# Dependencies that hold back loads of the front, wide fp32 products as TensorE's fillers, and an epsilon kept in a second column, in a kernel of attention, experts and slots

## The chip, the cores and the metric

The kernel runs on one core of a Trainium2 chip. Its engines are TensorE (PE, whose weight loads the profile lists as PEld), VectorE (DVE), ScalarE (ACT), GpSimd (POOL) and SyncE (SP), which here issues every transfer. The metric is the device time of one run in microseconds; lower is better. Of several runs the median counts.

## The reference

Three stages follow each other. Attention runs over 4 batches, 8 heads, 576 positions of 64 numbers and is the sum of two parts: one over queries, keys and values averaged over groups of 4 positions (144 of them), one over a band of positions less than 4 apart. Its output is a table of 2304 tokens by 512. A layer of width 2048 with a rational function follows, and then a soft mixture of 8 experts with 4 slots each.

```
def sm_attn(qq, kk, vv):
    s = scale * np.matmul(qq, kk.transpose(0, 1, 3, 2))
    s = s - np.max(s, axis=-1, keepdims=True)
    a = np.exp(s)
    a = a / (np.sum(a, axis=-1, keepdims=True) + 1e-09)
    return np.matmul(a, vv)
out_up = np.repeat(sm_attn(q_d, k_d, v_d), factor, axis=2)
attn_out = out_up + out_local              # out_local: banded, |i-j| < 4
...
h = x @ w_in
P = a[0] + a[1] * h + a[2] * h * h + a[3] * h * h * h
Q = 1.0 + np.abs(b[0]) * np.abs(h) + np.abs(b[1]) * h * h
x = (P / (Q + 1e-06)) @ w_out
...
logits = x @ phi
slot_input = softmax_over_tokens(logits).T @ x
slot_out[e] = np.maximum(slot_input[e] @ w1[e], 0.0) @ w2[e]
return softmax_over_slots(logits) @ slot_out
```

## The kernel before

Attention works on pairs of heads: 4 pairs for each of 4 batches, 16 in all. For a pair the program loads q and k (`load_qk`, L485, 579 KB) and two forms of v (`load_v`, L488: `vd` on 80 partitions with rows of 4 KB, `vw` on 112 partitions with rows of 5 KB). The averaged scores are made by `scd` on TensorE (L538), their peaks by VectorE (L543), the exponentials by ScalarE (L550), which also adds up each row into `dsm`; `norm_d` (L553) then adds the epsilon with a TENSOR_SCALAR (L555) and takes the reciprocal (L556). That holds for nine pairs; for the other seven the sum is a reduction of VectorE. The banded part has `sc` (L524, L528), a reduction (L561) and reciprocal (L562). `tp` and `tpd` (L572, L581) turn the exponentials, `av` and `avd` (L592, L599) multiply by v, ScalarE evicts (L603) and VectorE adds both parts (L616).

The weights of the wide layer come in pieces of 1 MB: eight of `w_in` (`load_in`, L691) and eight of `w_out` (`load_out`, L696). Each is split on VectorE into a high and a low part, in three steps per half or whole (L705, L710, L714). Four pieces of w_in and two of w_out come in the front, the others up to 130 us; products of w_out with the slot matrix are turned, multiplied and stored again (`wt` L772, `wp` L781, `wq` L791, `store` L767). The layer itself is `hps` (L838, L856), with its rational function over VectorE, ScalarE and GpSimd (L914 to L943), then slots and experts from about 411 us on, which stream 32 MB of expert weights.

What sets the order: all 1675 steps stand in a list with a time for each, written by hand (`PLACE`), and every engine's instructions follow that list. The class `Plan` walks over it with a cost for each part (`PARTS`) to choose two things: which PSUM bank a step gets, and how many fillers stand ahead of a step of TensorE for which it reckons with an idle gap. A filler is a product of zeros into a spare bank (`fillers`, L1105); it computes nothing. 48 of them open the program. All loads and the stores of w_out's product go through the one queue of SP in the order of the list. A load waits there when its buffer is still in use, and every load after the eighth also waits for an older transfer that used the same one of eight semaphores.

Names used below: "piece" is one load of w_in; "pair 0" is the first pair of the first batch, whose turn `tp` is the first in the program; a gate is a dependency of one load on another's landing.

Of the kernel before, what the change touches and what calls it, by code (L numbers as in the profile page):

```python
# [203 lines left out]
    dm=dict(pe=.216), coef=dict(dve=.85), roots=dict(act=.4), rooted=dict(dve=1.3), eps=dict(pool=.1),  # L204
    pq=dict(d=.7, p=[(1.62,)]), pk=dict(d=.7, p=[(1.73,)]), pv=dict(d=[(1.3,)], p=[(2.1,)]),
    sc=dict(pe=1.02), scd=dict(pe=.88), mx0=dict(dve=.5), mxd=dict(dve=.585), ms0=dict(act=.22), msd=dict(act=.22),
    ex0=dict(act=1.6), exd=dict(r=.8, s=1.2), nl=dict(dve=.69), nd=dict(r=("dve", .74), s=("dve", .34)),
    nlp=dict(d=[(.45,)], p=[(.8,)]), ndp=dict(d=[(.52,)], p=[(.87,)]),
    tp0=dict(pe=.455), tp1=dict(pe=.11), cp0=dict(act=.475), cp1=dict(act=.155),
    td0=dict(pe=.34), td1=dict(pe=.34), cd0=dict(act=.295), cd1=dict(act=.295), avd=dict(pe=.66), od=dict(act=.185),  # L210
    av=dict(pe=1.29), x20=dict(dve=.35), x21=dict(dve=.35), x8=dict(dve=.15),
    ldqk=dict(sp=1.5), ldv=dict(sp=3.4), ldi=dict(sp=2.75), ldo=dict(sp=2.75), sto=dict(sp=1.4), ldc=dict(sp=.6),
    w0=dict(dve=.7), w1=dict(dve=.67), w2=dict(dve=.62),
    ep=dict(act=.17), ri=dict(dve=.16),
    wih=dict(a=1.04, d=[(.6,)]), wil=dict(d=[(1.25,)], p=[(2.37,)]),
    wt0=dict(pe=.43), wt1=dict(pe=.4), wc0=dict(act=.48), wc1=dict(act=.48), wp=dict(pe=.57), wpp=dict(act=.265),
    wq=dict(pe=.42), wpc=dict(act=.11),
    xh=dict(a=.94, d=[(.6,)]), xl=dict(d=[(1.2,)], p=[(2.2,)]),
    h=dict(pe=2.72), h8=dict(pe=1.44), ab=dict(act=.92), cr=dict(a=1.15, d=[(.8,)], p=[(1.26,)], s=.98),
    v=dict(p=[(2.35,)], d=[(1.14,)]), a=dict(a=1.1, d=1.34), sq=dict(d=0.0, p=("act", .97)), t=dict(d=1.24, p=[(2.35,)]), p=dict(dve=1.2), ln=dict(act=1.06), ex=dict(act=.963),  # L220
    e=dict(dve=1.14), n=dict(dve=1.28), g=dict(d=[(1.25,)], f=1.16), tr=dict(pe=.435), gc=dict(a=.475, d=.605), lg=dict(pe=.57),
# [12 lines left out]
BLOCK, FIRST, AHEAD = 256, 445, 20  # L234
ENGINE = dict(a="act", s="act", r="act", d="dve", f="dve", p="pool")


class Plan:
# [37 lines left out]
    shared = dict(dve=.5, pool=.1)  # L276
    wait = dict(pe=.2, act=.14, dve=.13, pool=.14, sp=0.0)

    def fetch(self, now):
        queued = next((x for t, x in reversed(self.known) if t <= now), 0.0)  # L280
        return min(9.0, max(1.0, queued - now)) + 2.5

    def fetched(self, start, us, calls, times=1):
        us, calls, late = us * times, calls * times, 0.0
# [10 lines left out]

    def calls(self, n):
        x = self.items[n]
        if x[7] == "dm":
            return 4 * FILL[0]
        return int(CALLS[x[7]] * x[9][3] + .5)  # L300
# [8 lines left out]
    def simulated(self, banks):  # L309
# [4 lines left out]
        before, self.idles, read = None, {}, {}  # L314
        count, self.come, self.ran, self.sent = {}, {0: 14.4}, 0, []
        for x in items:
            count[x[7]] = count.get(x[7], -1) + 1
            x[0] = PLACE[x[7]][count[x[7]]]
# [6 lines left out]
        for n in done:  # L325
# [12 lines left out]
            if e == "sp":  # L338
                free[e] = t + .45 * self.issues.get(part, 1)
# [4 lines left out]
            if items[n][8]:  # L344
                us += self.shared[e]
            if e == "pe":
# [5 lines left out]

                if t - free[e] > .6:
                    self.idles[n] = int((t - free[e] - .35) / .11)
                us *= 1.02 if t > 5.3 else 2.0
                t = max(t, free[e] + self.fetched(free[e], .11, 2, self.idles.get(n, 0)))
                us = self.fetched(t, us, self.calls(n))
# [1169 lines left out]
```

## Time and profile before

| | us |
|---|---|
| median of 3 runs | 502.88 (502.02 to 504.41) |
| the profiled run | 501.73 |
| its span, first to last instruction | 499.8 |
| mean granted TensorE clock | 0.976 of full speed |
| TensorE busy | 463.7 (93%) |
| VectorE busy | 410.0 (82%) |
| ScalarE busy | 322.2 (64%) |
| GpSimd busy | 258.0 (52%) |

The busy shares are means over stages with different limits, so the stages have to be read apart: a front in which loads arrive (to about 53 us), a stretch with VectorE nearly full (to 120), a long one with TensorE nearly full (to 366), one with VectorE again (to 411), and the experts, which stream weights. The chain of waits goes back from the last instruction to what released each; "issue" in it is time in which the engine waited for nothing that the profile shows. In a timeline, square brackets give the idle time ahead of a row and what ended it.

### The profile page before, as it was taken

How to read it: one execution, taken by the hardware profiler on the slowest of the kernel's cores; microseconds unless marked ns; L12 is line 12 of the kernel's file. 1: busy time of each engine (PE TensorE's matmuls, PEld its weight loads, DVE VectorE, ACT ScalarE, POOL GpSimd, SP SyncE). 2: the span in 40 equal slices, each digit the busy share in tenths (PEclk: the TensorE clock that was granted, in tenths of full speed). 3: DMA queues.
4: the chain of work that ended last, by engine and by line, in shares of the span. 5: the costliest groups of instructions: out<-in, count | busy, mean ns of one | idle time of the engine just before them, and what ended most of it. 6: DMA issues, size and time to landing. Idle time of an engine off the chain costs nothing.

```text
span 499.8 us, 13199 instructions
## 1 busy us (share of the span) xinstructions
PE 463.7 (93%) x5562; PEld 342.9 (69%) x5562; DVE 410.0 (82%) x558; ACT 322.2 (64%) x676; POOL 258.0 (52%) x219
## 2 busy tenths in 40 slices
PE   8588979999999999999899999999999889989995
PEld 7466867676777777756677777677766678543674
DVE  5968999999997889889988989888889998825333
ACT  4675496686978877568598668869575657720222
POOL 3786779476982867574263477724643244401000
PEclk9578999999999999999999999999999999999998
DMA  8999617467645101034402222660202059999978
GB/s 330 299 302 298 257 49 211 169 217 224 211 122 159 55 26 49 12 110 122 122 1 65 58 75 82 218 243 1 84 1 84 1 199 353 380 412 424 427 320 309
DMA packets 17611, 88.52 MB, mean 177 GB/s; under 512 B 2064, under 2 KB 2576, under 8 KB 10896
## 3 DMA queue, kind: packets, MB, share of 16 engines
q1 hardware_dynamic: 17552, 87.67, 50.5%
q8 instruction: 44, 0.72, 0.6%
q14 instruction: 15, 0.12, 0.1%
HBM read 78.75 MB, written 8.91 MB: 175 GB/s over the span
## 4 chain that ended last, share of the span: by engine, by line
PE 51%; DVE 25%; ACT 9%; issue 5%; POOL 4%; DMA 4%; SPq 1%; DVEq 0%; ACTq 0%; POOLq 0%
PE hps L838 19%; PE op L1396 3%; DVE gate L939 3%; PE hp L1275 3%; PE gt L967 3%; PE av L592 3%; ACT hps L938 3%; DVE gate L943 2%; PE tpd L581 2%; POOL gate L920 2%; DMA at<-in_qk 2%; PE lg L983 2%; PE dsp L1039 2%; PE scd L538 2%; PE tp L572 2%
## 5 line engine op out<-in xcount | busy, mean ns | idle before, releaser
L838 PE MATMUL hps<-XH,W 128*128 128x512 f32 x512 | 168.2, 398 | 2.5 <-DVE A L942 1.4
L838 PEld LDWEIGHTS hps<-XH,W 128*128 128x128 f32 x512 | 96.1, 188 | 28.5 <-DVE A L942 3.7
L920 POOL TENSOR_TENSOR gate<-gate 128x1024 f32<-128x1024 f32 (+1 forms) x37 | 91.1, 2462 | 46.8 <-ACT gate L925 45.0
L838 PE MATMUL hps<-XL,W 128*128 128x512 f32 x256 | 100.0, 391 | 0.0
L916 POOL TENSOR_SCALAR gate<-gate,cf_sb 128x1024 f32<-128x1024 f32 (+1 forms) x25 | 30.7, 1227 | 81.8 <-ACT gate L924 81.8
L939 DVE SCALAR_TENSOR_TENSOR gate<-gate,hps 128x1024 f32<-128x1024 f32 (+1 forms) x37 | 44.0, 1189 | 20.5 <-ACT hps L938 17.6
L937 ACT ACTIVATE gate<-gate,one 128x1024 f32<-128x1024 f32 (+1 forms) x37 | 42.1, 1138 | 27.4 <-POOL gate L920 27.1
L838 PEld LDWEIGHTS hps<-XL,W 128*128 128x128 f32 x256 | 48.2, 188 | 8.9
L938 ACT ACTIVATE hps<-gate 128x1024 f32<-128x1024 f32 (+1 forms) x37 | 37.4, 1010 | 17.6 <-DVE A L936 8.5
L678 ACT COPY G<-gt 128x512 f32<-128x512 f32 x50 | 29.3, 590 | 6.8 <-PE gt L967 6.6
L967 PE MATMUL gt<-cf_sb,gate 128*128 128x128 f32 x192 | 28.7, 279 | 3.4 <-DVE G L680 1.4
L943 DVE SCALAR_TENSOR_TENSOR gate<-gate 128x1024 f32<-128x1024 f32 x17 | 30.7, 1807 | 0.4
L920 DVE TENSOR_TENSOR gate<-gate,hps 128x1024 f32<-128x1024 f32 x24 | 29.0, 1210 | 2.3 <-ACT gate L914 2.3
L924 ACT ACTIVATE gate<-hps 128x1024 f32<-128x1024 f32 (+1 forms) x26 | 25.9, 996 | 7.3 <-PE hps L838 6.4
L566 POOL TENSOR_TENSOR at<-at 128x342 f32<-128x342 f32 (+1 forms) x29 | 23.9, 832 | 10.9 <-PE tpd L581 3.4
L967 PEld LDWEIGHTS gt<-cf_sb,gate 128*128 128x128 f32 x192 | 21.4, 141 | 10.9 <-issue 4.7
L914 ACT ACTIVATE gate<-hps,cf_sb 128x1024 f32<-128x1024 f32 x23 | 27.9, 1213 | 1.1 <-PE lg L983 1.1
L936 DVE SCALAR_TENSOR_TENSOR gate<-gate,cf_sb,hps 128x1024 f32<-128x1024 f32 x22 | 28.1, 1275 | 0.5
L550 ACT ACTIVATE at<-sc,at 128x38 f32<-128x38 f32 x144 | 28.1, 316 | 0.4
L856 PE MATMUL hps<-xs,W 128*128 128x256 f32 x192 | 24.3, 285 | 3.2 <-DVE gate L942 3.1
L856 PEld LDWEIGHTS hps<-xs,W 128*128 128x128 f32 x192 | 23.3, 191 | 4.6 <-DVE gate L942 4.1
L518 POOL TENSOR_TENSOR at<-at 72x512 f32<-72x512 f32 x16 | 22.4, 1401 | 7.6 <-DMA at<-in_vd 7.6
(176 smaller groups left out, 1018.7 us busy)
## 6 DMA issues: line engine op xcount, KB each, us to landing
we<-in_w SPq DMA_DIRECT2D x32, 1024.0 KB, 11.3
at<-in_qk SPq DMA_DIRECT2D x16, 579.0 KB, 5.0
at<-in_vw SPq DMA_DIRECT2D x16, 560.0 KB, 6.9
wst<-in_w_in SPq DMA_DIRECT2D x8, 1024.0 KB, 15.4
wst<-in_w_out SPq DMA_DIRECT2D x8, 1024.0 KB, 5.7
at<-in_vd SPq DMA_DIRECT2D x16, 320.0 KB, 6.4
out<-late SPq DMA_DIRECT2D x17, 256.0 KB, 3.0
wo_dram<-wo SPq DMA_DIRECT2D x8, 512.0 KB, 6.6
```

The costliest lines, as they stand in the source:

```text
L550: nc.scalar.activation(out=dst[:, i, :], in_=st["s", j][:, i, :], func=ACTF.Exp, scale=scale, bias=mx[:, i:i + 1], accum_out=None if sums ...
L678: nc.scalar.copy(out=out, in_=x)
L838: nc.tensor.matmul(hps[m][:, c].rearrange("p u t -> p (u t)"), lhsT=W[p][:, w, kk, 128 * c:128 * c + 128], rhs=x[xx][:, kk, :], start=(kk ...
L856: nc.tensor.matmul(out[:, c, :], lhsT=W[p][:, w, kk, 128 * c:128 * c + 128], rhs=xs[i][:, xx, kk, :], start=(kk == 0 and j == 0), stop=(kk ...
L916: (nc.vector if who == "d" else nc.gpsimd).tensor_scalar(out=out, in0=x, scalar1=coef[:, w:w + 1], scalar2=coef[:, b:b + 1], op0=ALU.mult, ...
L920: (nc.vector if who == "d" else nc.gpsimd).tensor_tensor(out=out, in0=x, in1=y, op=op)
L936: stt(out=A, in0=A, scalar=coef[:, 1:2], in1=H, op0=ALU.add, op1=ALU.mult))
L937: do("ln", "C", "B", lambda C, B: act(out=C, in_=B, func=ACTF.Ln, bias=one))
L938: do("ex", "H", "C", lambda H, C: act(out=H, in_=C, func=ACTF.Exp, scale=-1.0))
L939: do("e", "B", "H", lambda B, H: stt(out=B, in0=B, scalar=1.0 + 1e-6, in1=H, op0=ALU.add, op1=ALU.mult))
L943: do("g", "A", "B" + n, lambda A, B, n: stt(out=A, in0=B, scalar=-2.0, in1=n, op0=ALU.add, op1=ALU.mult), pick=("g", m))
L967: nc.tensor.transpose(gt[n][:, u, 128 * c:128 * c + 128], g_of(n, c)[:, 128 * u:128 * u + 128], idn)
```

## The change

Four things change; the list of steps does not, so that every engine's instructions other than fillers keep their order.

Loads: every transfer is issued by `begin`. For the parts ldqk, ldv, ldi and ldo the planner goes back over the loads ahead until these add up to 2.6 us of its own cost, and makes the load wait until the one before those has landed. That gives 45 gates.

```diff
+BACK, LIMIT, GATED = -1.0, 2.6, ("ldqk", "ldv", "ldi", "ldo")
...
             if e == "sp":
+                ahead = 0.0
+                for m in reversed(loads if part in GATED else ()):
+                    if ahead >= LIMIT:
+                        t, self.gate[n] = max(t, end[m] + .1), m
+                        break
+                    ahead += items[m][2][0]
+                loads.append(n)
...
+    def begin(out, in_):
+        x = nc.sync.dma_start(out=out, in_=in_)
+        if plan.gate.get(plan.item) in begun and plan.item not in begun:
+            tc.add_manual_dep(x.ins, begun[plan.gate[plan.item]].ins.name, GATE, reason="few loads at once")
+        begun[plan.item] = x
...
     def load_qk(s, bb, p):
-        nc.sync.dma_start(out=s.qk, in_=qk[bb, p])
+        begin(out=s.qk, in_=qk[bb, p])
```

Fillers: a wide one is an fp32 product of 96 columns by 256, a narrow one now has 96 columns in place of 128. The planner's costs (`PARTS`) and its model of code fetches and of the port shared by VectorE and GpSimd change too, which moves fillers and PSUM banks only. 202 narrow fillers become 31 narrow and 57 wide; TensorE's instructions go from 11124 to 11010.

```diff
+    wide = zero.bitcast(F32)
-    def fillers(n):
+    def fillers(n, w=0):
+        for _ in range(w):
+            nc.tensor.matmul(fill[0:96], lhsT=wide, rhs=wide[:, 0:1].to_broadcast([128, TB]), start=not used, stop=True, skip_group_check=True)
+            used.append(n)
         for _ in range(n):
-            nc.tensor.matmul(fill[:, 0:192], lhsT=zero[:, 0:128], rhs=zero, start=not used, stop=True,
+            nc.tensor.matmul(fill[0:96, 0:192], lhsT=zero[:, 0:96], rhs=zero, start=not used, stop=True,
                              skip_group_check=True)
             used.append(n)
...
-        at(-100, "DM", "dm", fillers, 2 * FILL[0], w=["id"], scale=FILL[0])
+        at(-100, "DM", "dm", fillers, 0, FILL[0] // 2, w=["id"], scale=FILL[0])
```

The places, as narrow before and narrow/wide after: the first fill 48 to 0/6; ahead of the banded scores of a pair 5 to 1/1; ahead of the turn of pair 0 none to 2/7; ahead of its avd none to 0/2; a turn of w_out 2 to 3/0; then 14 to 3/3, 20 to 0/5, 20 to 0/5, 21 to 1/5 and 35 to 3/7; six new ones between 110 and 400 us (2/0, 2/0, 2/3, 0/2, 1/1, 2/3); in the tail 37 in six places to 9/7.

Epsilon: the row sums of the averaged scores go to the first of two columns of a new tile `dsa`, whose second was set to the epsilon at the start, and `norm_d` adds each pair by a reduction. That concerns nine pairs and adds four settings on GpSimd ahead of the first load's use.

```diff
         def norm_d():
             if F["sd"][index] == "s":
-                nc.vector.tensor_scalar(out=s.dsm, in0=s.dsm, scalar1=EPS, scalar2=None, op0=ALU.add)
-                nc.vector.reciprocal(out=s.dsm, in_=s.dsm)
+                norm(s.dsa, s.dsm)
...
         def norm(x, sm):
             nc.vector.tensor_reduce(out=sm, in_=x, axis=AX.X, op=ALU.add)
             nc.vector.reciprocal(out=sm, in_=sm)
```

A fourth, `turned_over`, lets a step of GpSimd wait for one of VectorE where the planner finds one that ended just before; with `BACK` at -1.0 it finds none, and no dependency is added.

On SP, at the program's start, the transfers stand as follows before (in_cb holds constants, in_qk one pair's q and k, in_cf more constants):

```order
1 L1118 DMA cb_sb<-in_cb 128x470
2 L486 DMA at<-in_qk 128x1158 x2
3 L691 DMA wst<-in_w_in 128x2048
4 L423 DMA cf_sb<-in_cf 128x390
5 L486 DMA at<-in_qk 128x1158 x2
6 L696 DMA wst<-in_w_out 128x2048
7 L691 DMA wst<-in_w_in 128x2048 [waits DMAHW0_49]
8 L489 DMA at<-in_vd 80x1024 [waits DMAHW1_49]
9 L490 DMA at<-in_vw 112x1280 [waits DMAHW2_49]
```

and after:

```order
1 L427 DMA cb_sb<-in_cb 128x470
2 L427 DMA at<-in_qk 128x1158 x2
3 L427 DMA wst<-in_w_in 128x2048 [waits DMAHW0_49]
4 L427 DMA cf_sb<-in_cf 128x390
5 L427 DMA at<-in_qk 128x1158 [waits DMAHW2_49]
6 L427 DMA at<-in_qk 128x1158
7 L427 DMA wst<-in_w_out 128x2048 [waits DMAHW4_49]
8 L427 DMA wst<-in_w_in 128x2048 [waits DMAHW6_49]
9 L427 DMA at<-in_vd 80x1024 [waits DMAHW7_49,DMAHW1_49]
10 L427 DMA at<-in_vw 112x1280
```

The order is the same; before, the first wait for an older load stands at the ninth transfer, now at the fourth, and the ninth waits for the seventh in place of the first.

On TensorE, from the last score product ahead of the first turn to the first av, before:

```order
121 L528 MATMUL sc<-at 32x38 x36
122 L581 MATMUL tpd<-cf_sb,at 72x128 x3
123 L572 MATMUL tp<-cf_sb,at 102x128 x4
124 L538 MATMUL scd<-at 64x144 x6
125 L599 MATMUL avd<-at 64x144 x4
126 L572 MATMUL tp<-cf_sb,at 38x128
```

and after (`lg<-zero` are the fillers):

```order
19 L580 MATMUL sc<-at 32x38 x36
20 L632 MATMUL tpd<-cf_sb,at 72x128 x3
21 L1159 MATMUL lg<-zero 96x256 x7
22 L1162 LDWEIGHTS zero
23 L1162 MATMUL lg<-zero 96x192
24 L1162 LDWEIGHTS zero
25 L1162 MATMUL lg<-zero 96x192
26 L623 MATMUL tp<-cf_sb,at 102x128 x4
27 L590 MATMUL scd<-at 64x144 x6
28 L1159 MATMUL lg<-zero 96x256 x2
29 L650 MATMUL avd<-at 64x144 x4
30 L623 MATMUL tp<-cf_sb,at 38x128
```

Nothing of the attention moved; nine fillers stand ahead of the first turn and two ahead of avd.

On VectorE, at the first epsilon, before:

```order
15 L561 TENSOR_REDUCE at<-at 128x9
16 L562 RECIPROCAL at<-at 128x9
17 L555 TENSOR_SCALAR at<-at 128x3
18 L556 RECIPROCAL at<-at 128x3
19 L561 TENSOR_REDUCE at<-at 128x9
```

and after:

```order
15 L612 TENSOR_REDUCE at<-at 128x9
16 L613 RECIPROCAL at<-at 128x9
17 L612 TENSOR_REDUCE at<-at 128x3
18 L613 RECIPROCAL at<-at 128x3
19 L612 TENSOR_REDUCE at<-at 128x9
```

The TENSOR_SCALAR has become a reduction in the same place.

## Rows read from the trace of the kernel before

**Rows 1.** Windows by stage: us, busy time by engine (instructions), clock, DMA share, GB/s.

```profile
53.00:120.00 67.00, 61.32 (x653) 48.04 (x646) 64.90 (x91) 48.76 (x91) 50.19 (x39) 1.00 0.52 169
120.00:366.00 246.00, 241.80 (x2938) 180.76 (x2937) 217.16 (x272) 185.86 (x392) 143.85 (x117) 1.00 0.31 98
...
411.00:450.00 39.00, 36.23 (x312) 24.17 (x310) 26.02 (x39) 22.09 (x45) 11.64 (x8) 1.00 0.97 383
```

**Rows 2.** Timeline of VectorE, 30 to 56 us: start, duration, instruction, idle before.

```profile
35.07 0.61 DVE L543 TENSOR_REDUCE at<-scd 128x3 f32<-128x432 f32 x1 [3.23 <-PE scd L538]
...
43.60 1.23 DVE L705 TENSOR_SCALAR nar<-wst 128x1024 int32<-128x1024 int32 x1 [0.57 <-DMA wst<-in_w_in]
...
48.33 0.42 DVE L616 TENSOR_TENSOR at<-av,at 128x256 f32<-128x256 f32 x1 [0.89 <-ACT at L603]
...
49.15 0.69 DVE L705 TENSOR_SCALAR nar<-wst 128x512 int32<-128x512 int32 x1
...
53.49 0.42 DVE L616 TENSOR_TENSOR at<-av,at 128x256 f32<-128x256 f32 x1 [0.66 <-ACT at L603]
```

**Rows 3.** Line L705, 0 to 60 us: VectorE's queue waits, first and last start.

```profile
L705 DVEq EVENT_SEMAPHORE  x4: 21/21/21, 21.8 to 49.1; - x4
```

**Rows 4.** Chain of waits, 0 to 60 us: start, duration, what.

```profile
16.25 0.86 PE tpd L581 x3
...
18.41 2.73 issue
...
22.52 0.87 PE tp L572 x4
...
28.58 1.10 issue
...
39.63 2.07 issue
```

**Rows 5.** Windows from the end of one stall to the next; columns as above.

```profile
21.10:29.60 8.50, 6.86 (x126) 5.16 (x125) 7.74 (x18) 5.72 (x25) 6.25 (x8) 0.70 1.02 296
29.60:41.65 12.05, 9.87 (x126) 7.43 (x126) 8.52 (x12) 6.48 (x18) 8.05 (x8) 0.76 1.03 272
```

**Rows 6.** Windows by granted clock (third number from the end).

```profile
14.90:25.10 10.20, 6.12 (x97) 4.52 (x99) 9.67 (x23) 5.46 (x21) 7.27 (x7) 0.50 1.03 270
...
28.50:35.40 6.90, 5.80 (x38) 4.43 (x37) 3.64 (x7) 4.33 (x8) 5.01 (x7) 0.51 1.04 309
```

**Rows 7.** Windows over a 1 MB load with vd and vw behind it, front and later.

```profile
31.00:39.11 8.11, 8.11 (x120) 6.17 (x119) 4.68 (x8) 5.59 (x17) 4.87 (x5) 0.73 1.04 256
...
76.40:79.65 3.25, 3.25 (x17) 2.73 (x16) 2.69 (x6) 1.99 (x6) 3.25 (x3) 1.00 0.97 380
79.65:82.70 3.05, 3.05 (x20) 2.03 (x18) 3.00 (x5) 2.15 (x3) 2.81 (x6) 1.00 0.67 186
```

**Rows 8.** DMA issues: count, KB each, median us to landing.

```profile
cb_sb<-in_cb SPq DMA_DIRECT2D x1, 117.5 KB, 2.1
```

**Rows 9.** Groups by line and form, TensorE: count, busy us, mean ns.

```profile
L1107 PE MATMUL lg<-zero 128*128 128x192 bf16 x202 | 20.9, 261 | 2.2 <-issue 1.1 <-DVE zero L1103 1.1
...
L1001 PE MATMUL lt<-LG,cf_sb 128*128 128x256 f32 x2 | 0.7, 431 | 0.0
```

**Rows 10.** Waits of TensorE, 120 to 366 us and 366 to 411 us.

```profile
PE gt L967 <- DVE G L680: 1.4, 1, 1.4
...
PE hps L856 <- DVE gate L942: 3.1, 2, 1.8
```

**Rows 11.** Groups by line and form, VectorE.

```profile
L555 DVE TENSOR_SCALAR at<-at 128x3 f32<-128x3 f32 x9 | 5.1, 565 | 0.1
...
L1012 DVE TENSOR_REDUCE peaks<-peaks 128x1 f32<-128x2 f32 x8 | 1.2, 155 | 0.3
```

**Rows 12.** Chain of waits, 113 to 122 us.

```profile
117.71 1.11 DVE at L555
```

**Rows 13.** Timeline of TensorE, 119 to 124 us.

```profile
119.65 0.64 PE L572 MATMUL tp<-cf_sb,at 128*102 128x128 f32 x4 [0.44 <-DVE G L680]
```

More of the change, by code (lines that the diff above doesn't have):

```diff
@@ L275 @@
     issues = dict(ldv=2, wor=4)
-    shared = dict(dve=.5, pool=.1)
+    gate, after = {}, {}
     wait = dict(pe=.2, act=.14, dve=.13, pool=.14, sp=0.0)
@@ L280, in fetch, with fetched @@
         queued = next((x for t, x in reversed(self.known) if t <= now), 0.0)
-        return min(9.0, max(1.0, queued - now)) + 2.5
-    def fetched(self, start, us, calls, times=1):
-        us, calls, late = us * times, calls * times, 0.0
+        return max(1.0, queued - now) + 2.5
+    def fetched(self, start, us, calls):
+        late = 0.0
+        if not calls:
+            return us
         for k in range(max(-1, (self.ran - FIRST) // BLOCK), (self.ran + calls - FIRST) // BLOCK + 1):
@@ L294, in fetched, with work, gap @@
         return us + late
+    def work(self, t, us):
+        return us * (2.0 if t <= 5.3 else 1.0)
+    def gap(self, start, us):
+        unit = [x * self.work(start + .1, 1.0) for x in (.43, .11)]
+        wide = int((us - .35) / unit[0])
+        return int((us - .35 - wide * unit[0]) / unit[1]), wide
     def calls(self, n):
@@ L313, in simulated @@
         owner, moved, self.place = [None] * banks, 0.0, {}
-        before, self.idles, read = None, {}, {}
+        before, self.idles, read, ports = None, {}, {}, dict(dve=[], pool=[])
         count, self.come, self.ran, self.sent = {}, {0: 14.4}, 0, []
+        self.gate, loads = {}, []
+        self.after = {}
         for x in items:
@@ L343, in simulated @@
                 continue
-            if items[n][8]:
-                us += self.shared[e]
+            if items[n][8] and e != "sp":
+                for a, b, _ in ports["pool" if e == "dve" else "dve"][-12:]:
+                    if a <= t + .1 and b > t:
+                        t = b
+                for a, b, _ in ports["pool" if e == "dve" else "dve"][-12:]:
+                    if t < a < t + us:
+                        us += t + us - a
+                        break
+                if e == "pool":
+                    last = [x for x in ports["dve"][-12:] if t - BACK < x[1] <= t]
+                    self.after[n] = last[-1][2] if last else None
+                ports[e].append((t, t + us, n))
             if e == "pe":
@@ L366, in emit @@
         for n in self.order(banks):
-            self.now = self.place.get(n)
+            self.now, self.item = self.place.get(n), n
             if n in self.idles:
-                self.idle(self.idles[n])
+                self.idle(*self.idles[n])
             self.items[n][5](*self.items[n][6])
@@ L390, in attn_moe_moe_kernel, with turned_over @@
     at = plan.at
+    begun = {}
+    def begin(out, in_):
[3 more added lines that the diff above has]
+        begun[plan.item] = x
+    met, told = {}, set()
+    def turned_over(x, who):
+        if who == "d":
+            met[plan.item] = x
+        elif plan.after.get(plan.item) in met and plan.item not in told:
+            tc.add_manual_dep(x.ins, met[plan.after[plan.item]].ins.name, GATE, reason="one of both engines at a time")
+            told.add(plan.item)
     def bank(name, shape=(512,)):
```

84 lines of the change are left out of this document (44 added, 40 removed).

## The prediction

> **What bounds the kernel now.** I read the windows by stage first. From 53 to 120 us VectorE is busy 64.90 of 67.00 us, from 120 to 366 us TensorE is busy 241.80 of 246.00, and from 411 to 450 us the DMA engines are busy 97% of the time [rows 1]. So a late start or an early finish of the front, 0 to 53 us, passes on in full through VectorE, whose order is fixed; a thing that only TensorE has to do before 120 us costs nothing unless VectorE waits for it.
>
> Second, VectorE's own timeline in the front. After the first q,k pair is in, it waits 3.23 us at 35.07 for a score product of TensorE, 0.57 us at 43.60 for the load of the fourth piece of w_in, 0.89 us at 48.33 and 0.66 us at 53.49 for ScalarE's evictions [rows 2]. That is 5.35 us, and no edit of the front can give more. Between the last two stands the fifth piece of w_in: VectorE takes its first step on it at 49.15, without idle time, but its last wait for a load is told at 49.1 [rows 3], so that load landed only just in time.
>
> Third, why TensorE is late at 35: the chain of waits has "issue" pieces of 2.73 us at 18.41, 1.10 at 28.58 and 2.07 at 39.63, in which TensorE waits for nothing that the profile shows [rows 4]. From one of them to the next the counts of TensorE's instructions (products and weight loads) are nearly equal: 126+125=251 and 126+126=252 [rows 5]. I read them as the fetch of the next block of instructions, itself a DMA behind the loads. Each stall also has a second price: the granted clock is 0.50 from 14.90 to 25.10 and 0.51 from 28.50 to 35.40, that is the 1.2 GHz level [rows 6]; it rose at 25.1 after TensorE had worked on from 21.14, and fell again with the next stall.
>
> Fourth, the loads. DMA is busy all through the front, yet from 31.00 to 39.11 it moves only 256 GB/s. In that stretch one piece of w_in with a vd and a vw load behind it arrives, in 8.11 us. Later in the kernel the same three kinds of load, with nothing more queued behind them, take 3.25+3.05=6.30 us, the second part with engines only 67% busy [rows 7]. So the deep queue costs about 1.8 us for each of the three such triples ahead of the fifth piece of w_in, some 5 us.
>
> **The change part by part.**
>
> *Gates.* 45 loads now wait until an older load has landed; up to the fifth piece of w_in there are twelve gates, later ones are met long before their load's turn. SP's order is kept, so behind a waiting load the whole of SP's queue waits: the next loads, and the store of wo that shares the queue. While it waits, by the planner, 2.6 us of loads or more are still under way. What a gate can cost: the smallest load, cb, took 2.1 us from issue to landing [rows 8]. That with an issue of some 0.4 us is 2.5 us, just under the 2.6 us. So I take no gap between loads, and keep up to 0.5 us per gate for the range. What the gates can give: the fetches are no longer behind 10 loads. I take 2.73, 1.10 and 2.07 as gone, and keep that they stay for a rival.
>
> Here a rule weighs against this reading. The rows show stalls of 1.10 to 2.73 us under a full queue [rows 4], but no fetch time under a short one. The Trainium skill, "DMA: Bandwidth & Descriptors", section "Queues, rings and completion order", says that each DMA engine alternates between its queues packet by packet. By that a fetch waits for a packet of the loads, not for all of them, and a shorter queue of loads would leave the stalls where they are. Then the sum lacks its first term, which is the second rival below.
>
> *Fillers.* Before, 202 narrow bf16 products took 20.9 us, about 0.10 each; the nearest row for a wide fp32 one is the 128x256 product of L1001, 431 ns [rows 9]; half the clock doubles it. Most places exchange like for like (20 narrow, 2.0 us, to 5 wide, 2.2 us). The tail has 37 narrow, now 9 narrow and 7 wide (3.8 against 3.9 us), beside a bound of DMA [rows 1]: nothing. The first fill of 48 is shorter and ends while the loads are awaited: nothing.
> The place that matters is the new fill of 7 wide and 2 narrow ahead of the first turn (tp) of pair 0, on the path to the product that VectorE awaits at 35.07. Before, that turn began at 22.52 [rows 4]. Without the stall TensorE would be there at 22.52-2.73=19.79. The fill lasts 7 x 0.43 + 2 x 0.10 = 3.2 us at full clock, 6.4 at half. The clock should rise earlier than at 25.1, since TensorE then works on without a stall from 16.25, where the chain enters it [rows 4]; if it rises by the same 2.73 earlier, at 22.4, the fill does 1.3 us of its work at half clock and 1.9 at full, and the turn begins at 24.3; with a full clock from the start at 23.0. I take 23.8, +1.3.
> From there to 35: the turn itself at full clock -0.4, two wide fillers ahead of avd +0.4 (0.9, of which I take 0.5 to lie beside ScalarE's part of that chain), the stall of 1.10 gone, one filler more +0.1. The work from 28.58+1.10=29.68 to 35.07 is 5.4 us at half clock; it would be 2.7 at full if all of it were columns; I take -1.9. Sum: 1.3-0.4+0.4+0.1-1.1-1.9 = -1.6. With the fill wholly at half clock (+3.7), 0.9 for the two and no gain by clock the sum is +3.6, with the best of each -3.5 (but VectorE can use only 3.23).
> So VectorE's wait goes from 3.23 to 1.6. Next in line are the loads. If the fourth and fifth piece of w_in land some 2 us earlier or more, as the shorter queue allows, the 0.57 goes as well, and about half of 0.89+0.66, since TensorE is ahead there by the stall of 2.07: 1.6+0.57+0.75 = 2.9 us.
> The new fillers in the middle: 3 and 2 wide ones stand where TensorE waits 1.4 us for VectorE anyway, or in the stretch from 366 to 411 where it waits 3.1 us at L856 [rows 10]; what lies open is a few narrow ones and part of a wide: +0.3 (0 to 1.4).
>
> *Epsilon.* Nine TENSOR_SCALAR of 565 ns become TENSOR_REDUCE over pairs; the nearest is the 128x2 reduction of L1012, 155 ns [rows 11]. That is -3.7 us of VectorE, but only what lies on the path counts. After 120 us TensorE bounds. In the front those ahead of 35.07 only lengthen the wait there: nothing. One is left: at 117.71 it took 1.11 us, and after it comes the eviction for which TensorE's turn at 119.65 waits [rows 12]. That wait is 0.44 us [rows 13], so the gain is 0.44, not 1.0. A reduction that takes as long as the TENSOR_SCALAR gives 0. Four memsets more on GpSimd lie ahead of the first load's landing: nothing. The dependencies for GpSimd (`turned_over`) never arise with these numbers, and PSUM banks change from 210 us on only by exchange: 0, and +-0.3 for the range.
>
> Sum: -2.9 (front) -0.44 (epsilon) +0.3 (fillers) = -3.0 us. The profiled run took 501.73 us with a span of 499.8, 1.15 under the median of 502.88; the sum is a difference, and I put it on the median: 499.9 us.
>
> **The rivals.**
> 1. *The loads hold VectorE.* The gates leave the loads' rate as it is, since vd and vw are slow by their own form. Then the fourth piece still lands at 43.6 and the fifth at 49.1, VectorE loses at them what it gained at 35.07, and of the front only 0.66 is left: -0.66-0.44+0.3 = -0.8, 502.1 us. For it: DMA is busy all through the front, and the sum of bytes is unchanged. Against it: the late triple of [rows 7].
> 2. *The fetches stay.* Stalls as before, with the new fill on top: the turn of pair 0 comes 1 to 3 us later than 22.52, the clock stays at half; VectorE's wait at 35.07 grows by about 1, and is given back at 43.6 and 49.1, where it had 0.57+0.89 of slack: the end is -0.44+0.3+0.3, 503.0 us. For it: the rule above. Against it: from 120 to 366 us, with a short queue, 5875 of TensorE's instructions pass and no "issue" wait is among its waits [rows 1, 10].
> 3. *The queue runs dry.* Slower. A gate that opens 0.5 us too late leaves the DMA engines idle for that long, twelve times up to the fifth piece of w_in: 6 us, of which the shorter queue may give 1 to 2 back. That load then lands at about 53.5 in place of 49.1, and VectorE, which was there at 49.15, is 4 us late less the 0.66 behind it: +3.4-0.44+0.3 = +3.2, 506.1 us. It decides from the point where the gaps together exceed what the unmixed loads give back. For it: 2.5 against 2.6 us is a thin margin. Against it: vd and vw take longer than the planner's numbers as yet, which widens it.
>
> That the change does not do what it says is part of the first two: gates without effect on the rate or on the fetch.
>
> **How the numbers follow.** Forecast 0.45, rival 1 0.25, rival 2 0.17, rival 3 0.13. About 0.5%, 2.5 us, is what a measurement of this kernel can tell from no change: faster is under 500.4, slower above 505.4. The forecast's own range is 497.8 (all 5.35 but 0.3 of the front) to 501.0; a tenth of it lies within 0.5% rather than beyond, as a tenth of rival 1 lies on the other side, so faster is 0.44, the same 0.44, slower 0.12. The range of 497.8 to 503.6 takes in the forecast and the first two rivals, and leaves the third and the best front outside.
>
> **What would show it.** Right: no "issue" piece over 0.5 us before 50 us in the chain; granted clock 1.00 from about 23 us on; VectorE's wait for the score product near 35 us at 1.6 us or less, and no wait of its for w_in; the window of a piece of w_in with vd and vw near 6.3 us; the epsilon reduction at 117 near 0.16 us and TensorE's wait at 119.65 gone. Wrong: DMA share well under 1 before 45 us (rival 3), the fill before the turn of pair 0 lasting 5 us or more, a wait of VectorE for w_in at 43 or 49 us (rival 1), "issue" pieces that stay (rival 2).

## The result, and the profile after

The changed kernel is slower: 504.96 us (median of 20 runs, 502.76 to 507.75) against 501.95 of the kernel before on the same chip (20 runs, 499.19 to 504.41), a ratio of 1.0054 with a 95% interval of 1.0037 to 1.0070, so +1.9 to +3.5 us. The prediction of 499.9 us (497.8 to 503.6) had the wrong sign. Runs more than 1.5% above the fastest of their kernel count as slow and are left out of the ratios below: two of e1_gates (505.24 and 508.49 us) and one each of e4_gates_eps, f1_no_mid, f5_gates_eps_rooted and h1_limit_5 (507.40 to 508.28), all of them kernels with gates. The profiled run of the changed kernel took 503.19 us, 1.8 under its median; its span is 501.4.

VectorE's timeline of the front, columns as in [rows 2], the same instructions (the line numbers are 51 or 52 higher):

```profile
34.00 0.61 DVE L595 TENSOR_REDUCE at<-scd 128x3 f32<-128x432 f32 x1 [0.43 <-PE scd L590]
...
42.49 1.23 DVE L756 TENSOR_SCALAR nar<-wst 128x1024 int32<-128x1024 int32 x1 [0.51 <-DMA wst<-in_w_in]
...
48.25 0.69 DVE L756 TENSOR_SCALAR nar<-wst 128x512 int32<-128x512 int32 x1 [1.14 <-DMA wst<-in_w_in]
...
51.76 0.42 DVE L667 TENSOR_TENSOR at<-av,at 128x256 f32<-128x256 f32 x1
...
52.61 0.54 DVE L496 SCALAR_TENSOR_TENSOR turns<-turns 128x2 f32<-128x2 f32 x1
...
53.38 0.17 DVE L495 RECIPROCAL turns<-turns 128x2 f32<-128x2 f32 x1
53.58 0.76 DVE L496 SCALAR_TENSOR_TENSOR turns<-turns 128x2 f32<-128x2 f32 x1
54.38 2.35 DVE L497 SCALAR_TENSOR_TENSOR turns<-turns 128x2 f32<-128x2 f32 x1
```

The wait for the score product has gone from 3.23 to 0.43 us, the two for ScalarE are gone, and the addition that stood at 53.49 comes at 51.76: the front did gain 1.73 us. Then come six tiny operations on the tile `turns` (square roots of two coefficients, `rooted`). Three of them take 0.54, 0.76 and 2.35 us. GpSimd's timeline beside it:

```profile
51.28 0.57 POOL L562 TENSOR_TENSOR at<-at 128x144 f32<-128x144 f32 x1 [2.19 <-DMA at<-in_qk]
51.93 1.20 POOL L564 TENSOR_TENSOR at<-at 128x144 f32<-128x144 f32 x2
53.24 1.09 POOL L734 TENSOR_TENSOR XL<-at,XH 128x512 fp32r<-128x512 f32 x1
54.28 2.43 POOL L734 TENSOR_TENSOR W<-wst,W 128x1024 fp32r<-128x1024 f32 x1
```

The three end at 53.15, 54.34 and 56.73, the last three of GpSimd's rows at 53.13, 54.33 and 56.71. Each of these tiny operations lasted until a GpSimd operation was over. In the trace of before only the last of the six was held up (the other five took 0.16 or 0.17 us), by XL and not by W; VectorE's row and GpSimd's:

```profile
55.14 0.94 DVE L447 SCALAR_TENSOR_TENSOR turns<-turns 128x2 f32<-128x2 f32 x1
```
```profile
51.94 0.57 POOL L510 TENSOR_TENSOR at<-at 128x144 f32<-128x144 f32 x1 [0.41 <-DMA at<-in_qk]
...
54.98 1.09 POOL L683 TENSOR_TENSOR XL<-at,XH 128x512 fp32r<-128x512 f32 x1 [1.18 <-ACT XH L678]
```

With that the front's gain was lost: VectorE, 1.74 us ahead at 53.5, is 0.65 us behind at 56.7.

The waits of TensorE up to 60 us, and TensorE's timeline at the new fill ahead of the first turn:

```profile
PE sc L580 <- issue: 1.6, 1, 1.6
```
```profile
19.92 4.72 PE L1159 MATMUL lg<-zero 128*96 128x256 f32 x14
24.47 0.33 PE L1162 MATMUL lg<-zero 128*96 128x192 bf16 x2
24.64 0.60 PE L623 MATMUL tp<-cf_sb,at 128*102 128x128 f32 x4
```

One "issue" stall of 1.6 us is left of the 2.73+1.10+2.07=5.90 in [rows 4]. A wide filler leaves two records, so 7 of them show as x14. The fill took 4.9 us, and the turn began at 24.64, 2.1 us later than in [rows 4]. The granted clock stood at half for the first 3.06 us of it and at full behind that (a window, columns as in [rows 1]):

```profile
19.92:22.98 3.06, 3.06 (x9) 2.06 (x9) 2.96 (x12) 1.82 (x10) 2.52 (x2) 0.50 0.98 289
```

Windows from 14 to 48 us, columns as in [rows 1], first of the kernel before and then of the changed one:

```profile
14.00:48.00 34.00, 26.03 (x483) 20.32 (x482) 28.23 (x47) 20.74 (x68) 24.11 (x26) 0.70 1.02 288
```
```profile
14.00:48.00 34.00, 29.87 (x483) 22.13 (x483) 29.14 (x52) 22.05 (x72) 27.11 (x29) 0.90 0.94 304
```

TensorE's granted clock rose from 0.70 to 0.90 of full speed. The DMA share fell from 1.02 to 0.94: the loads now have holes, although the rate rose from 288 to 304 GB/s. One such hole stands where the fifth piece of w_in, let go by the landing of the fourth, is issued at 42.53:

```profile
42.53:43.56 1.03, 1.03 (x58) 0.99 (x51) 1.03 (x1) 0.95 (x2) 0.01 (x1) 1.00 0.66 138
```

VectorE's waits for w_in up to 60 us come to 2.6 us, against the 0.57 of [rows 2]:

```profile
DVE nar L756 <- DMA wst<-in_w_in: 2.6, 3, 1.1
```

Later on. VectorE's waits from 53 to 120 us have a new first line, for a store of w_out's product whose buffer VectorE writes again; 1.1 us more are lost at it, at 115 us:

```profile
DVE wo L765 <- DMA wo_dram<-wo: 1.1, 1, 1.1
```

The epsilon, VectorE's timeline at 119 us and the group of all nine by line and form:

```profile
119.38 0.15 DVE L612 TENSOR_REDUCE at<-at 128x3 f32<-128x6 f32 x1
```
```profile
L612 DVE TENSOR_REDUCE at<-at 128x3 f32<-128x6 f32 x9 | 1.3, 147 | 0.1
```

That is what [rows 11] and [rows 12] led to expect (155 ns, 1.11 us gone at this place). And a fill of the middle, in TensorE's timeline:

```profile
325.80 0.64 PE L1034 MATMUL lg<-gate,wphi 128*32 128x256 f32 x8
326.37 1.11 PE L1159 MATMUL lg<-zero 128*96 128x256 f32 x4
327.13 0.58 PE L889 MATMUL hps<-XH,W 128*128 128x512 f32 x1
```

Ahead of the fill and behind it TensorE does not wait; the layer's product follows at 327.13 and not at the end of the product `lg`, 326.44. The stretch from 120 to 366 us, to set beside [rows 1]:

```profile
120.00:366.00 246.00, 244.03 (x2960) 182.32 (x2958) 212.75 (x272) 185.48 (x394) 143.69 (x117) 1.00 0.31 100
```

To follow a difference through the program I subtract, for the same VectorE instruction (their order is the same in all kernels here), its end in one trace from its end in the trace of before. Minus is earlier. The column heads are the runs below.

```
before us  after  e1_gates e2_fillers e4_gates_eps f2_rooted f3_rooted_no_mid g3_no_gates h1_limit_5  instruction
  35.07    -1.07   -1.94    -1.90      -1.38        -1.04     -3.19            -0.89       -1.24      peak of scd
  49.15    -0.91   -2.12    -1.79      -1.20        -0.75     -1.80            -1.92       -1.45      fifth piece of w_in
  53.49    -1.74   -2.95    -2.61      -2.03        -3.43     -4.48            -2.68       -2.28      addition
  56.73    +0.65   -0.56    -2.61      +0.36        -1.80     -3.41            -2.68       -2.26      next piece
 100.21    +0.64   -0.54    -2.66      +0.35        -1.47     -1.57            -2.69       -2.27      reduction
 119.52    +1.24   -0.55    -1.51      -0.16        -1.59     -0.86            -1.97       -2.31      layer
 230.20    +1.47   -0.69    -1.35      +0.13        -0.93     -0.68            -1.11       -1.53      addition
 241.00    -0.09   -1.01    -2.90      +0.06        -2.47     -2.23            -2.66       -3.08      addition
 334.19    +2.07   -1.01    -0.71      +1.45        -0.33     -2.11            -0.44       -0.88      layer
 430.42    +1.83   -1.01    -0.97      +0.91        -0.52     -2.16            -0.69       -1.13      experts
```

In f2_rooted and f3_rooted_no_mid the six tiny operations stand ahead of 53.49, so that 1.2 us of the gain in that one row is only their place. One trace is one execution: its end differs from the median of its kernel by up to 2.9 us, so the columns show where time goes, and the ratios what a kernel costs.

### The profile page after: what moved, and what is told of

It reads as the page before. It is cut to its first block, busy times and chain, and to the rows that moved or that the text cites. A ratio compares the mean times of both kernels' runs of the same rounds, so it can differ in the third digit from the quotient of the medians.

```text
span 501.4 us, 13094 instructions
## 1 busy us (share of the span) xinstructions
PE 473.0 (94%) x5505; PEld 343.9 (69%) x5505; DVE 406.8 (81%) x558; ACT 322.0 (64%) x676; POOL 257.9 (51%) x223
## 4 chain that ended last, share of the span: by engine, by line
PE 50%; DVE 21%; DMA 12%; ACT 8%; POOL 4%; issue 3%; SPq 1%; DVEq 0%; ACTq 0%; POOLq 0%
PE hps L889 20%; DMA wst<-in_w_in 5%; PE gt L1018 4%; POOL gate L971 3%; PE hp L1330 3%; PE lg L1034 2%; DVE gate L994 2%; DVE gate L990 2%; DMA at<-in_qk 2%; ACT hps L989 2%; PE dsp L1090 2%; PE op L1451 2%; PE av L643 2%; PE hps L907 2%; DMA wo_dram<-wo 2%
## 5 line engine op out<-in xcount | busy, mean ns | idle before, releaser
L889 PEld LDWEIGHTS hps<-XL,W 128*128 128x128 f32 x256 | 48.2, 188 | 9.9 <-POOL XL L734 1.0
L1159 PE MATMUL lg<-zero 128*96 128x256 f32 x114 | 32.4, 428 | 1.1 <-DVE zero L1154 1.1
L1159 PEld LDWEIGHTS lg<-zero 128*96 128x96 f32 x114 | 19.8, 184 | 11.1 <-issue 3.9
```

The lines of the kernel that those rows point to most:

```text
L889: nc.tensor.matmul(hps[m][:, c].rearrange("p u t -> p (u t)"), lhsT=W[p][:, w, kk, 128 * c:128 * c + 128], rhs=x[xx][:, kk, :], start=(kk ...
L1159: nc.tensor.matmul(fill[0:96], lhsT=wide, rhs=wide[:, 0:1].to_broadcast([128, TB]), start=not used, stop=True, skip_group_check=True)
```

## The experiments

Most start from the changed kernel and put parts of before back; `self.idles` is the list of fillers, `self.place` the PSUM banks, `self.gate` the gates.

**e1_gates: the gates alone.** Fillers, banks and epsilon of before:

```diff
+        self.idles = {22: (48, 0), 109: (5, 0), 153: (2, 0), 456: (14, 0), 157: (20, 0), 330: (21, 0), ...}
+        self.place.update({...})
...
         def norm_d():
...
-                norm(s.dsa, s.dsm)
+                nc.vector.tensor_scalar(out=s.dsm, in0=s.dsm, scalar1=EPS, scalar2=None, op0=ALU.add)
+                nc.vector.reciprocal(out=s.dsm, in_=s.dsm)
```

> The kernel before with the 45 gates alone (fillers, banks and epsilon as before). Theory A (the gates shorten TensorE's stalls, VectorE reaches 53 us about 1.7 us earlier, and then six tiny operations on the tile turns lose it, because they meet GpSimd there): VectorE ahead by 1 to 2 us at its addition of 53.5 us, level or behind by up to 1 us at 57, whole time within 1 us of before. Rival B (the gates leave holes in the loads and cost by themselves): VectorE behind already at 49 us, +2 us or more. Rival C (the gates are a gain that the other parts spoil): -1.5 us or better at the end.

Measured 0.9996 (0.9965 to 1.0027). VectorE's timeline and GpSimd's, where theory A put the loss:

```profile
52.08 1.06 DVE L499 SCALAR_TENSOR_TENSOR turns<-turns 128x2 f32<-128x2 f32 x1
53.17 2.35 DVE L500 SCALAR_TENSOR_TENSOR turns<-turns 128x2 f32<-128x2 f32 x1
```
```profile
52.02 1.09 POOL L737 TENSOR_TENSOR XL<-at,XH 128x512 fp32r<-128x512 f32 x1 [0.39 <-ACT XH L732]
53.08 2.43 POOL L737 TENSOR_TENSOR W<-wst,W 128x1024 fp32r<-128x1024 f32 x1
```

The first of the two began 0.06 us after GpSimd's XL and was held until XL was over; by then W had begun, and the second was held until W was over. Theory A holds as to the place: ahead by 2.95 us at 53.5, by 0.56 at 56.7. The gates are no cost and no gain by themselves that these runs can tell.

**e2_fillers: the new fillers alone.** As above with the fillers of after, and with

```diff
+        self.gate = {}
```

> The kernel before with the new fillers alone (31 narrow and 57 wide at the new places; no gates, banks and epsilon as before). Theory A (the fillers in the middle lie on TensorE's path: 1.7 us at 241 and 1.1 us at 326 in the trace of after): +1 to +2.5 us, nearly all of it gained after 230 us; in the front the fill ahead of the first turn adds nothing to VectorE's wait at 35 us or up to 2 us, which the loads at 43 and 49 us take back. Rival (fillers stand in idle time only): within 0.5 us of before.

Measured 1.0023 (0.9995 to 1.0050), in theory A's direction but not clear of none. Two things stand in the trace. Without any gate VectorE is 2.61 us ahead at 53.5, with "issue" stalls of 1.8 us in place of 5.9: for the front's gain the gates were not needed. The loads too come at 318 GB/s between 14 and 48 us, against 304 in the changed kernel. And from 241 to 334 us it loses 2.2 us, as the changed kernel does.

**e3_eps: epsilon alone.** The edit is the change's third part.

> The kernel before with epsilon in a second column alone (no gates; fillers and banks as before). Theory: the reduction at 117 us takes 0.16 us in place of 1.19, TensorE's wait at 119.65 goes, -0.4 us, and not more than -1.0. Rival (shifting VectorE by 1 us only moves a collision with GpSimd to the next operation): within 0.2 us of before.

Measured 1.0001 (0.9973 to 1.0030). The reduction took 0.15 us at 118.36 and VectorE gained 1.03 us there, of which 0.5 were lost again within 2 us. The expected 0.4 us is below what the runs can tell.

**e4_gates_eps: the changed kernel with the fillers and banks of before.**

> The changed kernel with the fillers and banks of before (gates and epsilon are in). Theory A: the sum of gates alone and epsilon alone, so within 1 us of before or up to 1 us faster, and 1.5 to 3 us faster than the changed kernel. Rival B (gates cost by themselves): +1.5 us or more against before, as slow as the changed kernel.

Measured 1.0022 (0.9994 to 1.0050): worse than the sum of its parts, though within their intervals, and 1.6 us under the changed kernel; between theory A and rival B it does not decide. The last tiny operation took 2.36 us here too.

**f1_no_mid: no fillers in the six new middle places.**

The six entries that stood between 470 and 1444 are left out:

```diff
+        self.idles = {22: (0, 6), 109: (1, 1), ..., 330: (1, 5), 470: (3, 7), 1444: (2, 1), 1505: (3, 1), ...}
```

> The changed kernel without its six new places of fillers between 110 and 400 us (11 narrow and 11 wide less); gates, front fillers, banks and epsilon stay. Theory A (the fillers at 241 and 326 us lie on TensorE's path): 1 to 2 us faster than the changed kernel, so +0.7 to +2 us against before, the gain arising at about 241 and 326 us in VectorE's times. Rival (those places are idle anyway): as the changed kernel, +2.7 us.

Measured 1.0028 (1.0001 to 1.0055), in theory A's span, 1.3 us under the changed kernel with an uncertainty of the same size. Its profiled run took 507.97 us, 5.0 over the median, and is not read.

**f2_rooted: the tiny operations moved** ahead of VectorE's step at 49.7 us, where GpSimd is idle.

```diff
-    rooted=(188,),
+    rooted=(179.5,),
```

> The changed kernel with the six tiny operations on the tile turns moved ahead of VectorE's step at 49.7 us, where GpSimd stands idle. Theory A (the gates' gain of the front is lost because these operations meet GpSimd's): each of the six at 0.15 to 0.2 us, VectorE ahead of before by 1.5 to 2 us still at 57 us, and 1.5 to 2.4 us faster than the changed kernel, so about +0.5 us against before. Rival (the loss only moves to another meeting on VectorE or to the loads at 54 to 59 us): as the changed kernel.

Measured 1.0037 (1.0003 to 1.0072): 0.9 us under the changed kernel, about half of what theory A expected, and not clear of it. The trace shows the edit at work: the first and the last of the six take 0.16 us,

```profile
49.74 0.16 DVE L498 RECIPROCAL turns<-turns 128x2 f32<-128x2 f32 x1
...
50.72 0.16 DVE L500 SCALAR_TENSOR_TENSOR turns<-turns 128x2 f32<-128x2 f32 x1
```

and VectorE is 1.80 us ahead at 56.7 instead of 0.65 behind. The collision is therefore real, but by the times it is not the whole loss.

**f3_rooted_no_mid: both edits.**

> Both edits in the changed kernel: tiny operations moved, and no fillers in the six new places. Theory A: the two gains add, 2.5 to 4 us faster than the changed kernel, -1.5 to 0 us against before. Rival (one of the two does nothing): as the better one of the two alone.

Measured 0.9989 (0.9956 to 1.0021), 3.3 us under the changed kernel: the two together undo the loss, as theory A said, although the gates are still in (DMA share 0.97, 3.4 us of VectorE's waits for w_in). From 241 to 334 us VectorE now loses nothing (-2.23 and -2.11).

**f4_before_rooted: the same move in the kernel before.**

> The kernel before with only the tiny operations on turns moved ahead of VectorE's step at 49.9 us. Theory A: the one of them that took 0.94 us in the trace of before takes 0.16, so -0.5 to -0.8 us; if the move alone gives 1.5 us or more, it is no meeting that the gates brought about. Rival (nothing to gain in before): within 0.3 us.

Measured 1.0021 (0.9989 to 1.0054): theory A's 0.5 to 0.8 us did not show. The move is no gain that these runs can tell where only one of the six operations waited.

**g3_no_gates: the changed kernel without its gates.** The one line that counts is `self.gate = {}`; fillers, banks and the list of steps are those of the changed kernel.

> The changed kernel without its 45 gates (fillers, banks and epsilon stay). Theory D (the gates leave small holes in the loads, make the run-to-run spread larger, and let the tiny operations on turns meet GpSimd): 0.5 to 1.5 us faster than the changed kernel, so +1.2 to +2.2 us against before, DMA busy 1.0 all through the front, VectorE ahead by 2 to 3 us at 53.5 us and still ahead by 1.5 us or more at 57. Rival (the gates are what brings the front forward): VectorE at 53.5 us level with before, and slower than the changed kernel.

Measured 0.9987 (0.9963 to 1.0010), 3.4 us faster than the changed kernel, and the two intervals are apart: in the changed kernel as it stands, the loss needs the gates. VectorE's timeline, GpSimd's beside it, the window from 14 to 48 us and the waits for w_in up to 60 us:

```profile
52.46 0.95 DVE L500 SCALAR_TENSOR_TENSOR turns<-turns 128x2 f32<-128x2 f32 x1
```
```profile
52.29 1.09 POOL L737 TENSOR_TENSOR XL<-at,XH 128x512 fp32r<-128x512 f32 x1 [0.50 <-ACT XH L732]
```
```profile
14.00:48.00 34.00, 30.00 (x483) 22.49 (x485) 28.89 (x52) 21.70 (x70) 26.58 (x27) 0.90 1.02 316
```
```profile
DVE nar L759 <- DMA wst<-in_w_in: 0.5, 1, 0.5
```

No holes, the clock as with gates, one tiny operation waiting as before, and VectorE ahead by 2.68 us at 53.5 and at 56.7. That is what theory D expected of the trace. The time went further than it said: 3.4 us and not 0.5 to 1.5 under the changed kernel, level with before and not 1.2 to 2.2 us over it.

**g4_old_banks: the changed kernel with the banks of before.**

> The changed kernel with the PSUM banks of before (77 choices from about 210 us on go back). Theory (the banks do nothing): as the changed kernel, +2 to +3.4 us against before. Rival (the part of the loss that no single part of the change shows lies in the banks): 1 us or more faster than the changed kernel, with a wait of TensorE for an eviction after 210 us that is gone.

Measured 1.0048 (1.0026 to 1.0069), the changed kernel's loss: the banks are not the cause. Its profiled run, 505.17 us, is nearer to what the changed kernel mostly takes than the 503.19 read above. In it VectorE waits 4.5 us for w_in up to 60 us and is already 0.99 us behind before at the fifth piece, 0.16 behind at 53.5, and 2.53 behind at 56.7, after the same three tiny operations (0.51, 0.79 and 2.34 us). So in this run the holes took the front's gain before the collision did its part.

**g1_fill_no_gates_moved: the best of the parts.** No gates, no middle fillers, tiny operations moved.

> No gates; the new fillers of the front and the tail but none in the six new middle places; epsilon in the second column; the tiny operations on turns ahead of VectorE's step at 49.7 us. If the fillers of the front alone bring VectorE forward, and the two losses (middle fillers, tiny operations) are the ones named: 1.5 to 3 us faster than before, and as fast as or faster than the same with gates (-0.6 us). If the gates are needed for the front: within 0.7 us of before.

Measured 0.9976 (0.9950 to 1.0002), 500.79 us against 502.00: the fastest, 1.2 us under the kernel before though not quite clear of it, and 3.9 us under the changed one by the ratios. Of the 1.5 to 3 us that I expected it falls short.

**f5_gates_eps_rooted: gates and epsilon with the old fillers, tiny operations moved.**

> Gates and epsilon with the fillers and banks of before, and the tiny operations on turns moved. Theory A (the gates' gain of the front is kept where those operations meet nothing): 0.5 to 2 us faster than before, and about 1.5 us faster than the same with the operations unmoved (+1.1 us). Rival D (the gates' holes eat what they give): within 0.7 us of before, with a spread of runs as wide as the other kernels with gates.

Measured 1.0016 (0.9989 to 1.0043). Theory A fell here, and rival D is the nearer (+0.8 us): with nothing to collide, the gates still gave nothing. The window shows the holes at their largest:

```profile
14.00:48.00 34.00, 27.10 (x495) 20.97 (x496) 28.71 (x50) 20.88 (x70) 25.21 (x27) 0.80 0.89 276
```

VectorE waited 3.7 us for w_in in three places. The runs spread from 499.73 to 508.28 us.

**h1_limit_5: gates that leave twice as much under way.**

```diff
-BACK, LIMIT, GATED = -1.0, 2.6, ("ldqk", "ldv", "ldi", "ldo")
+BACK, LIMIT, GATED = -1.0, 5.2, ("ldqk", "ldv", "ldi", "ldo")
```

> The changed kernel with its gates leaving twice as much under way (5.2 us of loads by the planner's costs in place of 2.6); all else stays. Theory E (the loss is the holes between loads, since 2.6 us is about the time from one load's landing to the first data of the load it lets go): DMA share 1.0 between 14 and 48 us, VectorE's waits for w_in under 1.5 us together, 1.5 to 3.5 us faster than the changed kernel, so -1 to +1 us against before. Rival F (any gate makes the loads meet the tiny operations on turns or the fetch differently, holes do not matter): within 0.7 us of the changed kernel, +2.5 us.

Measured 1.0018 (0.9993 to 1.0043), between the two theories: 1.8 us under the changed kernel, 1.6 over the one without gates, and clear of neither. The trace agrees with theory E: no holes,

```profile
14.00:48.00 34.00, 29.57 (x493) 21.91 (x493) 28.17 (x51) 21.56 (x70) 26.35 (x26) 0.95 1.02 314
```

1.2 us of waits for w_in, and only one tiny operation that waits (0.94 us). But the "issue" stalls are back at 4.8 us.

**h2_no_gates_no_mid: no gates and no middle fillers, tiny operations unmoved.**

> The changed kernel without gates and without fillers in the six new middle places; the tiny operations on turns stay where they are. Theory: the middle fillers cost 1 to 1.5 us of what the gateless kernel (-0.65 us) has, so -1.2 to -2.2 us against before; the move of the tiny operations alone is worth no more than 0.8 us here, since without gates only one of them waits. Rival (middle fillers are free): -0.65 us as without their removal.

Measured 0.9999 (0.9976 to 1.0022), not the 1.2 us or more that I expected. In this trace the front gave 1.52 us at 53.5 only, and 2.0 us were lost between 119 and 230, where the granted clock fell to half for 3.4 us (0.50 in the window from 213.7 to 217.1). So the times alone do not show that the middle fillers cost anything: without them the ratio fell by 0.0026 and 0.0048 where gates were in, and rose by 0.0012 where they were not.

## Why the prediction was wrong

**What bounds the kernel** was read rightly as to the stages: VectorE waits at the same places, the banks were worth nothing (g4_old_banks), and from 430 us to the end the changed kernel's trace loses nothing more. But that an early finish of the front "passes on in full through VectorE" did not hold: the 1.7 us ahead at 53.5 had become 0.65 us behind at 56.7, because VectorE met GpSimd there.

**The gates were the step that failed, in "So I take no gap between loads".** I had 2.5 us for a load to come (issue and [rows 8]) against 2.6 us that are still under way, and called that enough. The shares of DMA say otherwise: 0.94 to 0.97 between 14 and 48 us in six profiles with these gates (after, e1_gates, e4_gates_eps, f2_rooted, f3_rooted_no_mid, g4_old_banks), 0.89 in f5_gates_eps_rooted, and 1.02 in each of the kernels without gates or with twice the margin. From 1.02 to 0.94 over 34 us is 2.7 us of load time, by estimate 0.2 us for each of the twelve gates (of 46 in the program, not 45), inside the 0.5 us that I kept for the range; it is a mean, and the hole at 42.53 is larger. The better rate that I hoped for from a shorter queue is not the gates' work: with the new fillers it is 301 to 318 GB/s without gates and 294 to 305 with them, with the old fillers 288 to 294 without and 276 to 306 with them. The fifth piece of w_in came at 48.2 us and not 2 us earlier than 49.1. So the landings stayed nearly where they were, as rival 1 had it, with the mechanism of rival 3 behind them.

**What took the sign in the trace was not on my list of terms.** I worked out that VectorE would be early at 53.5, but not what it would meet there. The six tiny operations cost 0.8 us more in before than they do with nothing beside them, and 3.2 us more in the changed kernel; in all four profiles with these gates and the operations in their old place that I read (after, e1_gates, e4_gates_eps, g4_old_banks) the last one takes 2.34 to 2.36 us, in before, e2_fillers, e3_eps, g3_no_gates, h1_limit_5 and h2_no_gates_no_mid 0.94 or 0.95. What decides is whether XL catches the fifth of the six or only the sixth: behind the fifth, the sixth comes up when W is already running. That is a race of under 0.1 us. In h1_limit_5 the fifth came up at 52.69, as XL began, and took 0.16; in e4_gates_eps it came up 0.03 us after XL and took 1.08. In the changed kernel GpSimd's work on the next pair begins, after a wait for the gated q,k load, only 0.5 us ahead of VectorE's addition (51.28 and 51.76), in g4_old_banks too, where in g3_no_gates it is 0.9 ahead and in before 1.6 (51.94 and 53.49). But in e1_gates and e4_gates_eps it is 0.8 ahead, as in h1_limit_5 and h2_no_gates_no_mid, and the race was lost all the same. So that gates with 2.6 us of margin decide it fits all ten traces, but is argued and not shown. Moving them gave the 2.4 us back in the trace; in the times it was 0.9 us (f2_rooted), 2.0 from f1_no_mid to f3_rooted_no_mid, and 0.3 from e4_gates_eps to f5_gates_eps_rooted.

**The fetches.** I took the stalls as gone; 1.6 us stayed. They do depend on the queue: 1.3 to 2.4 us with the gates at 2.6 us of margin, 1.8 to 7.2 without them, and with the old fillers the two are apart (1.5 to 2.3 in e1_gates, e4_gates_eps and f5_gates_eps_rooted, 5.0 to 7.2 in before, e3_eps and f4_before_rooted). That speaks against the second rival and the rule that stood behind it. But the term was put down to the wrong part: the new fillers alone brought the stalls to 1.8 us in one trace and VectorE as far forward as the gates did.

**The new fill** took 4.9 us against 3.2 to 4.5 by my sum, since the clock rose late, at 23.0 and not at 22.4; the path to 35 us gained 1.07 us and not 1.6. **The middle fillers** were sized at +0.3 us (0 to 1.4). In the traces VectorE loses 2.2 us from 241 to 334 us with them in after, e2_fillers, f2_rooted, g3_no_gates, g4_old_banks and h1_limit_5, and 0.1 without them in f3_rooted_no_mid, g1_fill_no_gates_moved and h2_no_gates_no_mid. e4_gates_eps and f5_gates_eps_rooted, which have none of them, lose 1.4 there, but in both the granted clock fell to half for 3.4 us, in e4_gates_eps here:

```profile
241.00:244.50 3.50, 3.31 (x69) 1.87 (x73) 3.46 (x7) 1.67 (x2) 1.09 (x1) 0.51 0.00 0
```

So in the traces the middle fillers cost about 2 us; in the times, three pairs of kernels that differ in nothing else give 1.3, 2.4 and -0.6. **Epsilon** was right: 0.147 us each, 1.03 us at one place, about half of it kept.

The sum in the traces: -1.7 (front), +2.4 (tiny operations), +1.1 (the wait for the store at 115 us, which I had not foreseen either), -0.5 (epsilon), the rest on and off after 230 us, +1.8 us at the experts. That is the trace; the medians are 3.0 us apart, and the other 1.2 us the two profiled runs do not show. The wait for the store is not the gates' work: it is 1.3 us in g3_no_gates and 1.4 in e2_fillers, and there is none in before, e1_gates, e3_eps and e4_gates_eps.

**What stays open.** That the gates cost 3.4 us in the changed kernel is shown by g3_no_gates. It is no fixed price: five pairs of kernels differ in the gates alone, and there the gates cost 3.4 us (changed kernel and g3_no_gates), 1.5 (f1_no_mid and h2_no_gates_no_mid), 0.7 (f3_rooted_no_mid and g1_fill_no_gates_moved), 1.1 (e4_gates_eps and e3_eps) and -0.2 (e1_gates and before), only the first of them clear of zero. And f3_rooted_no_mid, with the gates in, undoes the loss as well. So gates, collision and middle fillers seem each to have a part, and how the loss divides among them is not settled: taking away the collision gave 0.9 us, holes and collision 1.8, each uncertain by about 1.5 or more.

## What to carry to other kernels

A limit on how many loads are under way needs a margin over the time from one landing to the next load's first data; where the two were equal on paper, the gates here left holes of some 0.2 us each by estimate, and the kernel without them was the faster one. Before an engine is made to arrive earlier, read what runs on the other engines at the new time: small operations beside GpSimd's long ones can take back more than was won. Fillers belong only in places that the trace shows idle; the planner's gaps of 0.6 us and more were not there at 326 us.

## What the runs showed of the hardware that was not expected

A VectorE operation on 128x2 numbers can take 2.35 us: it ends with GpSimd's TENSOR_TENSOR that was running when it came up (0.01 to 0.02 us apart, three times in the changed kernel), and takes 0.16 us when none runs. The Trainium skill, "SBUF — State Buffer", section "SBUF: two separate sides", says that VectorE and GpSimd share a port pair under an exclusive lock held for a whole instruction, and that a VectorE instruction with two inputs in SBUF contends there with a GpSimd one that reads SBUF; the three rows, with both inputs in `turns`, agree with that.

The traces also show what is not held up. The reciprocal at 53.38, with one input, took its usual 0.17 us under GpSimd's XL of 53.24 to 54.33. In e2_fillers, VectorE's integer SCALAR_TENSOR_TENSOR on w_in, which has one input in SBUF and the other (`nar`) in PSUM, took its usual 0.68 us, the first of them at 53.53 under GpSimd's W of 53.41 to 55.85; the group from 53.4 to 56 us, and W:

```profile
L769 DVE SCALAR_TENSOR_TENSOR wst<-wst,nar 128x512 int32<-128x512 int32 x2 | 1.4, 682 | 0.1
```
```profile
53.41 2.44 POOL L738 TENSOR_TENSOR W<-wst,W 128x1024 fp32r<-128x1024 f32 x1
```

The epsilon's gain is of the same kind. In before the TENSOR_SCALAR on 128x3 numbers ended 0.02 us after a GpSimd operation that had begun ahead of it, VectorE's row and GpSimd's:

```profile
117.62 1.19 DVE L555 TENSOR_SCALAR at<-at 128x3 f32<-128x3 f32 x1
```
```profile
117.51 1.28 POOL L518 TENSOR_TENSOR at<-at 72x512 f32<-72x512 f32 x1
```

In e3_eps the reduction in its place came up under the same GpSimd operation and took 0.15 us:

```profile
118.36 0.15 DVE L616 TENSOR_REDUCE at<-at 128x3 f32<-128x6 f32 x1
```
```profile
118.22 1.28 POOL L574 TENSOR_TENSOR at<-at 72x512 f32<-72x512 f32 x1
```
